# Nine warm-up products in place of eleven at the start of a mixer-and-MLP kernel

**The chip, the cores and the metric.** One core of one Trainium2 chip. The metric is device microseconds for one execution of the program. Engines: PE is TensorE's matmuls, PEld its weight loads, DVE VectorE, ACT ScalarE, POOL GpSimd, SP the engine that issues most DMAs. "Eleven" and "nine" stand for the kernel before and after.

## The reference, cut to what matters

```python
B, S, D, F = 1, 2048, 512, 1792                   # bf16
h  = gelu(layernorm(x) @ w1)                      # layer 1
hs = concat(four column groups of h, shifted by 1, -1, 2, -2 tokens) @ w2
x1 = x + hs
out = x1 + gelu(layernorm(x1) @ w3) @ w4          # layer 2
```

## The kernel before

Sixteen tiles of 128 tokens. A script fixes TensorE's order. The other engines' orders come from a list scheduler inside the kernel, with its own model of durations. The script begins:

```python
SCRIPT = """
warm:11 sa:0 sb:0 ty:1 ra:0 rb:0 ty:2 up1:1 th:0 up1:2 ty:3 mix:0-1 ty:5 ty:4 up1:3-4 ...
"""
LOADS = """
tp16 x1 x2 w1a w1b x3 x4-5 w2b w2a x8 x6 w3b w3a ... x0@act x12
"""
```

`warm:n` issues n products on a tile of zeros that nothing reads. `sa`, `sb` are the first and second pair of transposes of tile 0, each needing one normalised half of x. `ra`, `rb` are its four w1 products; the first two need the first half of w1 (`w1a`), the last two the second half (`w1b`). `ty:t` are transposes of tile t, `up1:g` the w1 product of a group, `th:0` the transposes back, `mix:t` the four w2 products of a tile.

```python
def warm_pe(n):
    b, v = next_bank()
    rows = zeros[:].unsqueeze(1).to_broadcast([P, 4, P])
    def f(e):
        for _ in range(n):
            ins = e.matmul(o_ps[:, b, :], zeros[:], rows, start=True, stop=True)
        return ins
    pg.add("pe", ..., f, reads=[(("zeros",), 0)], writes=[(("o", b), v)],
           dur=min(n, 7) * 427 + max(0, n - 7) * 216)          # the scheduler's model

# the four products of tile 0, in two halves (hh)
ins = e.matmul(y_ps[:, p, 0:D], xnT[:, dc, P*t : P*(t+1)], w1_sb[:, dc, :], start=(dc == 0), stop=(dc == DC-1))
# the mixing product of tile t
ins = e.matmul(dst, hT[:, j, c0 : c0+P], w2_sb[:, j, :], start=(j == 0), stop=(j == DC-1))
```

## Time and profile before

| | eleven |
|---|---|
| median of 3 runs | 135.48 us (135.25 to 135.73) |
| profiled execution | 135.97 us, span 134.6 us |
| TensorE busy | 132.4 us, 98% of the span |
| warm-up | eleven products, 0.44 to 5.1 us |
| full clock granted from | 6.44 us |
| layer 2's first product | 18.30 us |

The profiled execution is slower than the median: executions differ, and the first 10 us decide by how much. The last line is a good gauge, since from there TensorE runs nearly without a gap. Below, "start of layer 2" is that moment:

```profile
18.30 2.90 PE L641 MATMUL y_ps<-xnT,w_sb 128*128 128x128 bf16 x49
```

(From TensorE's timeline of eleven: start, length, what.) The lines that show the bound and the warm-up are in the prediction.

### The profile page before, as it was taken

What the parts mean: (1) busy time and instruction counts of PE and PEld (TensorE: products, weight loads), DVE (VectorE), ACT (ScalarE), POOL (GpSimd) and SP (SyncE); (2) the same over time, 40 slices, a digit from 0 to 9 for tenths busy, and PEclk for the clock granted to TensorE, in tenths of its full rate; (3) what the DMA queues carried; (4) which work ended last, traced back from release to release, by engine and by line L of the source; (5) the groups of instructions that cost most, each with busy time, mean ns of one, the idle gap of its engine ahead of it and who ended that gap; (6) DMA issues with size and microseconds to landing.
All of it is one profiled execution on the core that took longest, in us unless ns stands there. A gap on an engine that the chain in (4) does not pass through costs nothing.

```text
span 134.6 us, 2153 instructions
## 1 busy us (share of the span) xinstructions
PE 132.4 (98%) x847; PEld 73.1 (54%) x847; DVE 48.6 (36%) x147; ACT 62.1 (46%) x97; POOL 26.4 (20%) x61
## 2 busy tenths in 40 slices
PE   8999999999999999999999999999999999999994
PEld 3587779644656444444448844444444444444464
DVE  2689898863078810050007032232220000232222
ACT  6669829897544875557657542000006663000000
POOL 2444548963003650010003210000000000000000
PEclk9999999999999999999999999999999999999999
DMA  5999999955572135001000302111111000111112
GB/s 150 294 358 406 353 176 362 98 113 98 100 83 78 39 78 105 12 5 39 0 0 0 79 6 64 53 39 39 39 39 39 0 5 0 39 39 39 39 39 78
DMA packets 21369, 12.19 MB, mean 91 GB/s; under 512 B 13936, under 2 KB 20848, under 8 KB 21360
## 3 DMA queue, kind: packets, MB, share of 16 engines
q1 hardware_dynamic: 20784, 11.80, 35.0%
q10 hardware_dynamic: 576, 0.26, 0.7%
q8 instruction: 6, 0.10, 0.3%
q14 instruction: 3, 0.02, 0.1%
HBM read 6.82 MB, written 2.10 MB: 66 GB/s over the span
## 4 chain that ended last, share of the span: by engine, by line
PE 98%; DVE 0%; issue 0%; DVEq 0%
PE y_ps L641 46%; PE o_ps L710 36%; PE o_ps L681 10%; PE o_ps L735 4%; PE y_ps L505 2%; PE y_ps L543 1%; DVE o_sb L718 0%; PE o_ps L609 0%; DVE zeros L362 0%; DVEq L873 0%
## 5 line engine op out<-in xcount | busy, mean ns | idle before, releaser
L641 PE MATMUL y_ps<-xnT,w_sb 128*128 128x128 bf16 (+2 forms) x480 | 63.7, 292 | 0.0
L641 PEld LDWEIGHTS y_ps<-xnT,w_sb 128*128 128x128 bf16 x480 | 39.2, 98 | 24.2 <-DVE nmr L465 0.2
L710 PE MATMUL o_ps<-w_sb,h2T 128*128 128x512 bf16 (+3 forms) x252 | 48.9, 355 | 0.0
L656 ACT ACTIVATE h2T<-y_ps 128x1024 bf16<-128x1024 f32 (+2 forms) x29 | 28.7, 994 | 36.8 <-PE y_ps L641 36.8
L710 PEld LDWEIGHTS o_ps<-w_sb,h2T 128*128 128x128 bf16 x252 | 23.6, 98 | 25.2
L718 DVE TENSOR_TENSOR o_sb<-o_ps,x_sb 128x512 bf16<-128x512 f32 (+3 forms) x18 | 11.4, 631 | 43.3 <-PE o_ps L710 43.3
L681 PE MATMUL o_ps<-w_sb,hT 128*128 128x512 bf16 x64 | 15.4, 379 | 0.0
L438 POOL TENSOR_TENSOR rstd<-mv,neghalf 128x1 f32<-128x1 f32 x18 | 9.9, 554 | 26.8 <-DVE mv L433 25.0
L431 DVE BATCH_NORM_STATS2 st<-x_sb 128x6 f32<-128x512 bf16 x18 | 12.1, 675 | 2.7 <-DMA x_sb<-in_x_dram 2.7
L438 POOL TENSOR_TENSOR rstd<-vpe,neghalf 128x1 f32<-128x1 f32 x14 | 7.7, 557 | 26.2 <-DVE mv L420 14.1
L688 DVE SCALAR_TENSOR_TENSOR x_sb<-o_ps,x_sb 128x512 bf16<-128x512 f32 x10 | 6.9, 688 | 15.6 <-PE o_ps L681 15.6
L656 ACT ACTIVATE hT<-y_ps 128x512 bf16<-128x512 f32 (+1 forms) x10 | 8.1, 809 | 5.2 <-PE y_ps L641 5.2
L469 ACT ACTIVATE xn_buf<-x_sb,nmr,rstd 128x512 bf16<-128x512 bf16 x12 | 9.6, 806 | 1.9 <-POOL nmr L465 1.3
L415 ACT ACTIVATE junk<-x_sb 128x512 bf16<-128x512 bf16 x14 | 8.7, 623 | 3.7 <-DVE x_sb L688 3.4
L692 DVE TENSOR_TENSOR x_sb<-o_ps,x_sb 128x512 bf16<-128x512 f32 x6 | 4.1, 686 | 15.5 <-PE o_ps L681 15.4
L681 PEld LDWEIGHTS o_ps<-w_sb,hT 128*128 128x128 bf16 x64 | 6.1, 98 | 5.7 <-issue 0.2
L460 DVE TENSOR_SCALAR xn_buf<-x_sb,mv,rstd 128x512 bf16<-128x512 bf16 x12 | 5.3, 440 | 1.7 <-POOL rstd L438 1.3
L472 POOL TENSOR_SCALAR xn_buf<-x_sb,rstd,nmr 128x512 bf16<-128x512 bf16 x7 | 5.5, 784 | 0.6 <-DVE nmr L465 0.4
L735 PE MATMUL o_ps<-zeros 128*128 128x512 bf16 x11 | 4.9, 629 | 0.4 <-DVE zeros L362 0.4
L433 DVE BATCH_NORM_AGGREGATE mv<-st 128x2 f32<-128x9 f32 x18 | 3.2, 187 | 0.2
L505 PE MATMUL y_ps<-ident,xn_buf 128*128 128x128 bf16 x32 | 3.2, 242 | 0.0
L505 PEld LDWEIGHTS y_ps<-ident,xn_buf 128*128 128x128 bf16 x32 | 2.6, 110 | 1.1 <-issue 0.6
(34 smaller groups left out, 30.9 us busy)
## 6 DMA issues: line engine op xcount, KB each, us to landing
w_sb<-in_w_dram SPq DMA_DIRECT2D x4, 896.0 KB, 7.8
out_dram<-o_sb SPq DMA_DIRECT2D x15, 128.0 KB, 1.7
x_sb<-in_x_dram SPq DMA_DIRECT2D x9, 128.0 KB, 5.0
w_sb<-in_w_dram SPq DMA_DIRECT2D x4, 256.0 KB, 4.8
x_sb<-in_x_dram SPq DMA_DIRECT2D x3, 256.0 KB, 5.2
xnT<-xn_buf SPq DMA_TRANSPOSE x24, 2.5
x_sb<-in_x_dram ACTq DMA_DIRECT2D x1, 128.0 KB, 2.6
out_dram<-o_sb ACTq DMA_DIRECT2D x1, 64.0 KB, 1.6
```

Source lines behind the costliest of these rows:

```text
L415: (lambda d: (lambda e: e.activation(d, src, ACT_F.Square, accum_out=sums[:, q, 1:2])))(junk[:, b, :]),
L431: pg.add("dve", f"bnst{q}", lambda e: e.bn_stats(st9[:, q, 0:6], src), reads=rs, writes=[(("st", q), 0)], dur=605)
L438: lambda e: e.tensor_tensor(col(rstd), var, neghalf[:], ALU.pow),
L469: f = lambda e: e.activation(dst, src, ACT_F.Identity, bias=nmr[:, q : q + 1], scale=rstd[:, q : q + 1])
L505: ins = e.transpose(chunk(c), xn_buf[:, slot(q), P * c : P * (c + 1)], ident[:])
L641: ins = e.matmul(y_ps[:, p, W * i : W * (i + 1)], wsb[:, dc, P * fc : P * (fc + 1)], src[:, dc, P * t0 : P * t0 + W], start=(dc == 0), sto ...
L656: (lambda d, s: (lambda e: e.activation(d, s, ACT_F.Gelu_apprx_tanh)))(dst, ysrc),
L681: ins = e.matmul(dst, hT[:, j, c0 : c0 + P], w2_sb[:, j, :], start=(j == 0), stop=(j == DC - 1))
L688: f = lambda e: e.scalar_tensor_tensor(x1_sb[:, t, :], dst, 1.0, x_sb[:, t, :], ALU.mult, ALU.add, accum_out=sums[:, NT + t, 0:1])
L710: ins = e.matmul(dst, h2T[:, fc, P * t : P * (t + 1)], w4_sb[:, fc, cs], start=(fc == 0), stop=(fc == FC - 1))
L718: (lambda d, c: (lambda e: e.tensor_tensor(o_sb[:, oi, c], d, x1_sb[:, t, c], ALU.add)))(dst, cs),
L735: ins = e.matmul(o_ps[:, b, :], zeros[:], rows, start=True, stop=True)
```

## The change

Its intent: real work stands ready behind the last warm-up products, so let it in earlier.

```diff
-warm:11 sa:0 sb:0 ty:1 ra:0 rb:0 ty:2 up1:1 th:0 up1:2 ty:3 mix:0-1 ty:5 ty:4 up1:3-4 ty:6 mix:2 up1:5 ty:16
+warm:9 sa:0 sb:0 ty:1 ra:0 rb:0 ty:2 up1:1 th:0 up1:2 ty:3 mix:0-1 ty:5 ty:4 up1:3-4 ty:6 mix:2 up1:5 ty:16
```

## The prediction

> **What bounds the kernel now.** I read the page first (busy shares, then the chain that ended last), then the pieces of that chain in order of time, then the timeline of the first 10 us, because the change touches only the first instructions.
>
> The page's shares, its busy tenths for PE and its chain:
>
> ```profile
> PE 132.4 (98%) x847; PEld 73.1 (54%) x847; DVE 48.6 (36%) x147; ACT 62.1 (46%) x97; POOL 26.4 (20%) x61
> PE   8999999999999999999999999999999999999994
> PE 98%; DVE 0%; issue 0%; DVEq 0%
> ```
>
> TensorE is the bound from 0.44 us to the end: it alone is 98% of the chain, so a shift of its first real product moves the end by as much, unless a wait appears. The start of the chain, piece by piece (start, length, what):
>
> ```profile
> 0.44 4.87 PE o_ps L735 x11
> 5.31 0.85 PE y_ps L505 x8
> 6.17 1.06 PE y_ps L543 x4
> 7.23 0.22 PE y_ps L505 x4
> 7.45 0.89 PE y_ps L641 x16
> ```
>
> The first piece is the eleven warm-up products on zeros; nothing reads their result. Then come the transposes of tiles 0 and 1 (eight), four 512-column products for tile 0, the transposes of tile 2 (four) and the first w1 block. The weight loads give the issue spacing (start, length, what, idle before):
>
> ```profile
> 3.83 0.15 PEld L735 LDWEIGHTS o_ps<-zeros 128*128 128x128 bf16 x1 [0.28 <-issue]
> 4.26 0.15 PEld L735 LDWEIGHTS o_ps<-zeros 128*128 128x128 bf16 x1 [0.28 <-issue]
> 4.68 0.15 PEld L505 LDWEIGHTS y_ps<-ident,xn_buf 128*128 128x128 bf16 x1 [0.28 <-issue]
> 5.11 0.79 PEld L505 LDWEIGHTS y_ps<-ident,xn_buf 128*128 128x128 bf16 x7 [0.28 <-issue]
> ```
>
> They step by 0.427 us: all eleven products ran at the slow rate. The eleventh is issued at 4.68 and the first transpose product starts at 5.11. When were its operands there? The timeline again:
>
> ```profile
> 3.58 0.91 ACT L446 ACTIVATE xn_buf<-x_sb,mv 128x256 bf16<-128x256 bf16 x2
> 4.10 0.41 DVE L460 TENSOR_SCALAR xn_buf<-x_sb,mv,rstd 128x512 bf16<-128x512 bf16 x1
> 5.56 0.29 DVE L513 COPY xnT<-y_ps 128x256 bf16<-128x256 bf16 x1 [0.95 <-PE y_ps L505]
> 5.89 0.28 DVE L513 COPY xnT<-y_ps 128x256 bf16<-128x256 bf16 x1
> 6.16 0.41 DVE L460 TENSOR_SCALAR xn_buf<-x_sb,mv,rstd 128x512 bf16<-128x512 bf16 x1
> ```
>
> The two halves of tile 0 (ScalarE) ended at 4.08 and 4.49, tile 1 (VectorE) at 4.51. So the first transposes stood ready behind warm-up products for 0.6 to 1.0 us, and VectorE idled 0.95 us for them. That is what the change is after.
>
> **What the Trainium skill says.** "TensorE: Matmul & The Clock Gate", Part 1, says the array starts at half clock and is released after a busy window of about 3.4 us that runs freely, so the moment depends on where the first product falls in it; it gives 426.7 ns per 512-column product cold and 215.7 ns warm. The trace agrees: 427 ns for every warm-up product, 216 ns between the third and fourth tile-0 products. Its clock record starts full rate at 6.44 us, 6.0 us after the first product, and the spacing changes there. (The page's row of granted clock shows full speed throughout, having no earlier record.) The same page, Part 4, says transposes do not count as busy for this clock in the same way. Nothing here shows that: transposes fill 0.86 us of the 3.4 us before the release, and later ones run 56 ns apart, the full rate. I keep it as a risk.
>
> **The change part by part.** Two products go: 2 x 0.427 = 0.854 us of TensorE at the slow rate. The ninth then ends its issue at 0.441 + 9 x 0.427 = 4.28 instead of 5.11 to 5.14. That isn't the gain. The clock is released by time, not by count, so real work that moves forward moves into slow time. With the release at T and real work beginning at S before T, work worth (T-S)/2 of full-rate time is done at T, so the end goes as (T+S)/2: two products fewer are worth at most 0.854/2 = 0.43 us, whatever T is.
>
> Now with the waits of this trace, release kept at 6.44:
> 1. First two transposes of tile 0: ready 4.08, start 4.28, take 2 x 0.107, to 4.49.
> 2. Second two: the half ends at 4.48; with about 0.15 from an end to a TensorE start (the smallest slacks of this trace are 0.12 to 0.16) they start at 4.63. A new idle of 0.14. To 4.84.
> 3. Four of tile 1: ready, 4.84 to 5.27.
> 4. Tile-0 products 1 and 2 need the first copy (starts 4.73, ends 5.03) and half of w1, whose last piece landed at 5.08; TensorE itself is the latest, 5.27. At 0.427 each, to 6.12.
> 5. Products 3 and 4 need the other half of w1 (5.77) and the second copy (about 5.43): start 6.12. 0.32 us of the third is slow, its last quarter fast (0.05), then 0.216: to 6.71.
> 6. Tile 2's transposes start at 6.71 instead of 7.07; their operand (VectorE, behind both copies) ends near 5.83.
>
> Gain: 7.07 - 6.71 = **0.36 us**. Does it survive? I took the slack of each later TensorE block, its start less the end of its last operand. The tight ones are the transposes of the gelu of tile 0 (0.16), the w1 blocks of tile 2 (0.14) and tile 4 (0.12), and the first layer-2 transpose (0.13). All hang on ScalarE, VectorE and GpSimd work released by TensorE itself, which moves along. Fixed are the loads: tile 3 lands at 6.12 for statistics that began at 6.48 (room 0.36); the last of w2 at 8.96 for a product at 9.55, then 9.19 (0.23 left, about 0.1 after the hop); tile 6 at 9.61 for statistics at 10.05, then 9.69. From 18.3 us on slack is over 1 us at nearly every block (0.5 to 0.9 at three blocks from 36.7 to 40.1, fed by TensorE's own work; the tail pieces feed one another), so nothing later takes the gain back.
>
> In executions where the clock is released earlier, the gain is smaller. At T = 4.5 the eleven end at 4.83 and tile 2's transposes start near 6.44, held by copies and norms; with nine they start near 6.32, held by the second half of w1 (5.77 plus hop, then 2 x 0.216). That leaves 0.12, and w2 at 8.96 would take most of it. Between 0.1 and 0.36, I choose 0.25: 135.48 - 0.25 = 135.23, call it 135.25.
>
> **The rivals.**
> (a) *Loads take over and nothing is gained.* For: w1's second half and w2 are within 0.1 to 0.4 us of becoming the last operand. Against: in the profiled execution each still had room. Time 135.4 to 135.5.
> (b) *The clock is released a window later.* With nine products there is a hole of about 0.14 us near 4.5, and more of the deciding window is transposes. If that window no longer counts as busy, release slips about 3.4 us and the end by half, some 1.7 us less the 0.36: near 136.8. Against: the hole is 4% of the window. For: the first 2.6 us of products before 3.03, about three quarters of the window before the deciding one, did not release it, so some threshold above three quarters is possible. One in twelve.
> (c) *The list order of the other engines changes.* The kernel places instructions with its own model, in which the warm-up's length enters (products beyond seven at 216 ns: 0.43 us less). The order is tuned by a table of biases, so ScalarE, VectorE and GpSimd could be dealt differently. In that model, too, the second half of tile 0 holds TensorE, so later steps move little. For harm: slacks of 0.12 to 0.16 in the first 17 us. Against: over 1 us later. Plus or minus 0.3 us, rarely 1.
> (d) *The whole 0.85 us is gained*, if the release came earlier by as much. Against: nothing earlier is busy than before. 134.6.
>
> **Range and chances.** The three runs spread over 0.48 us, as a release at random times would make them (0.5 us per us of T); the median of a few moves by 0.2. Adding (a) to the upper side and (d) to the lower, and some of (b) and (c): 134.8 to 136.0. Two per cent is 2.7 us. A gain of that size exceeds all the products removed, and a loss needs (b) and a bad (c) together: faster 0.01, same 0.97, slower 0.02.
>
> **What would show each step right or wrong.** Nine weight loads of the warm-up 0.427 apart; the first transpose product near 4.28, a gap of 0.1 to 0.2 before the third, tile 2's transposes 0.1 to 0.4 us earlier at an equal release time; real products at 0.427 up to the release. The release should lie within 3.4 to 6.8 us of the first product; much later is (b). An idle stretch that a load ends, on TensorE near 5.8 or 9.0, is (a). A different sequence on VectorE or ScalarE is (c). I am wrong if equal release times give an equal or later end, or over 0.5 us gained.

## The result, and the profile after

Nine: 135.28 us median of 6 runs (135.20 to 135.41). Eleven beside it: 135.37 (135.01 to 137.26; the last is set aside as slow in the ratio, but counted in this median). The ratio is 0.9998, 95% interval 0.9978 to 1.0017: the same. A ratio here is the mean time of one kernel's runs over that of the other's of the same rounds, so it isn't quite the ratio of the medians quoted. Executions over 1.5% slower than the fastest of the same kernel are left out of the means.

Compared instruction by instruction, the orders of VectorE, ScalarE, GpSimd and SP are identical in both; on TensorE two products are missing. So rival (c), another order, is out.

The profiled execution of nine took 135.24 us, 0.73 less than that of eleven. That is *not* the effect of the change, as the weight loads show (start, length, what, idle before and what ended it):

```profile
3.41 0.15 PEld L735 LDWEIGHTS o_ps<-zeros 128*128 128x128 bf16 x1 [0.28 <-issue]
4.37 0.13 PEld L505 LDWEIGHTS y_ps<-ident,xn_buf 128*128 128x128 bf16 x2 [0.81 <-POOL rstd L438]
4.71 0.34 PEld L505 LDWEIGHTS y_ps<-ident,xn_buf 128*128 128x128 bf16 x6 [0.21 <-ACT xn_buf L446]
5.12 0.13 PEld L543 LDWEIGHTS y_ps<-w_sb,xnT 128*128 128x128 bf16 x2
5.68 0.11 PEld L543 LDWEIGHTS y_ps<-w_sb,xnT 128*128 128x128 bf16 x2 [0.43 <-DMA w_sb<-in_w_dram]
...
8.80 0.56 PEld L681 LDWEIGHTS o_ps<-w_sb,hT 128*128 128x128 bf16 x4 [0.20 <-issue]
```

Two things differ from eleven. First, the clock: in this execution it was released between 3.84 (the ninth warm-up product) and 4.41 us, since the first transposes already run 0.055 us apart; in the execution of eleven it was released at 6.44. Second, waits that eleven did not have. The weights of the third tile-0 product wait for w1 (last piece landed at 5.63). At 8.80 the first mixing product comes late too: TensorE's sequencer stands in a wait from 8.27 to 8.77 that ends with the last of w2 (landed at 8.74); the view says only "issue". So a gain was there and loads stepped into it.

A trap in reading: the page's chain of nine, and its first long pieces, name something else.

```profile
PE 91%; DMA 3%; DVE 2%; issue 1%
```

```profile
2.08 3.92 DMA x_sb<-in_x_dram
...
8.43 0.61 DVE st L431
9.04 1.67 PE o_ps L681 x7
```

(The first fence is the chain by engine, the second the chain in order of time.) It blames tile 3's load and the statistics of tile 4. But the line says x7 where two tiles of four products make eight: the record of the first mixing product is missing. Its weights were loaded at 8.80, so it started near 8.83, and the chain, starting from the second product at 9.04, took a VectorE instruction that had ended at 9.03 for its releaser. The mixing products read nothing from it.

Layer 2 began at 17.57:

```profile
17.57 3.62 PE L641 MATMUL y_ps<-xnT,w_sb 128*128 128x128 bf16 x62
```

From there to the end both executions are equal: 135.97 - 18.30 = 117.67 and 135.24 - 17.57 = 117.67. Whatever the change does, it does before 18 us.

### The profile page after: what moved, and what is told of

Read it like the earlier page. It is cut to its first block, busy times and chain, and to the rows that moved or that the text cites. A ratio compares the mean times of both kernels' runs of the same rounds, so it can differ in the third digit from the quotient of the medians.

```text
span 133.9 us, 2137 instructions
## 1 busy us (share of the span) xinstructions
PE 130.8 (98%) x833; PEld 72.3 (54%) x845; DVE 48.8 (36%) x147; ACT 62.3 (47%) x97; POOL 26.4 (20%) x61
## 2 busy tenths in 40 slices
DMA packets 21369, 12.19 MB, mean 91 GB/s; under 512 B 13936, under 2 KB 20848, under 8 KB 21360
## 4 chain that ended last, share of the span: by engine, by line
PE 91%; DMA 3%; DVE 2%; issue 1%
PE y_ps L641 45%; PE o_ps L710 36%; PE o_ps L681 10%; DMA x_sb<-in_x_dram 3%; DVE st L431 1%; PE y_ps L505 1%; DVE hT L619 0%; DVE mv L433 0%; DVE xn_buf L460 0%; DVE o_sb L718 0%; DVE xnT L513 0%
## 5 line engine op out<-in xcount | busy, mean ns | idle before, releaser
L681 PE MATMUL o_ps<-w_sb,hT 128*128 128x512 bf16 x58 | 14.3, 379 | 0.5 <-DVE st L431 0.3
L735 PE MATMUL o_ps<-zeros 128*128 128x512 bf16 x9 | 4.0, 631 | 0.4 <-DVE zeros L362 0.4
L427 DVE SCALAR_TENSOR_TENSOR vpe<-sums,mv 128x1 f32<-128x1 f32 x14 | 2.2, 158 | 2.7 <-ACT junk L415 2.4
L423 DVE TENSOR_SCALAR mv<-mv 128x1 f32<-128x1 f32 x14 | 2.9, 210 | 0.3
```

The source lines that it names most:

```text
L681: ins = e.matmul(dst, hT[:, j, c0 : c0 + P], w2_sb[:, j, :], start=(j == 0), stop=(j == DC - 1))
```

## The experiments

**Theory (loads).** Where the clock is released early, nine is held by w1's second half and w2, and the gain goes into that wait; where it is released late, nine is some 0.4 us ahead. **Rivals.** (norms) The two halves of tile 0's normalisation hold TensorE, no load does. (nothing) The products weren't on the path at all. (full) Each product costs its whole 0.427 us.

Twelve runs in three groups of four, each group on one chip (the first and the third on the same); eleven ran beside each group. In kernels with moved loads or foreign weights the compute engines' orders were kept as they were, and compared. The table has the profiled executions, in us. "Release" is where the spacing of products turns from 0.427 to 0.216 (or of transposes from 0.107 to 0.056), or the clock record where there is one; "w1" the landing of the last piece of its second half; "third" the start of the third tile-0 product.

| run | release | w1 | third | start of layer 2 | that less w1 | time |
|---|---|---|---|---|---|---|
| eleven (before) | 6.44 | 5.77 | 6.64 | 18.30 | 12.52 | 135.97 |
| nine (after) | 3.84-4.41 | 5.63 | 5.68 | 17.57 | 11.94 | 135.24 |
| nine_again | 3.51 | 6.28 | 6.33 | 18.00 | **11.72** | 135.77 |
| nine_third | 6.29 | 5.61 | 6.00 | 17.80 | 12.19 | 135.50 |
| nine_fourth | 6.30 | 5.61 | 5.95 | 17.78 | 12.18 | 135.44 |
| nine_free | 4.79 | 5.70 | 5.58 | 17.37 | 11.67 | 135.04 |
| eleven_free | 5.56 | 5.20 | 6.44 | 18.10 | 12.91 | 135.78 |
| thirteen | 3.89 | 6.14 | 6.19 | 17.86 | **11.72** | 135.67 |
| none | 7.03 | 5.13 | 5.69 | 17.98 | 12.84 | 135.67 |
| nine_x2act | 4.34 | 6.01 | 6.06 | 17.73 | **11.72** | 135.49 |
| eleven_x2act | 5.50 | 5.41 | 6.43 | 18.09 | 12.68 | 135.76 |
| nine_w1act | 3.64 | 4.25 | 6.54 | 18.20 | 13.95 | 135.87 |
| nine_latew1 | 5.76 | 6.79 | 6.83 | 18.50 | **11.72** | 136.17 |
| eleven_latew1 | 5.02 | 6.77 | 6.81 | 18.48 | **11.72** | 136.16 |

In bold: the third product waited for w1's second half, and no later load held.

The time less the start of layer 2 is 117.66 to 117.81 in all fourteen; the span (first to last instruction) less it is 116.34 to 116.35. So the start of layer 2 settles the span almost exactly, and the rest of the time lies outside the span.

Release and landing may not be independent. In the nine traces with w1's second half at its usual place, the two earliest releases known to 0.1 us (3.51 and 3.89) go with the two latest landings (6.28 and 6.14), and releases from 4.79 on with 5.13 to 5.77. That is too little to show a link, and no run sets the one without the other.

### First group: the change again, loads taken off the path, two products more

**nine_again** (no edit; the changed kernel).

> The changed kernel once more, beside eleven on the same chip. Loads theory (the gain is lost because the second half of w1, then the last of w2, become the last operand when the clock is released early): over 5 rounds 0.0 to 0.2 us under eleven, scatter smaller than that of eleven; TensorE waits for the w1 load before the third tile-0 product and for the w2 load before the first mixing product, unless the release is late (after 5.5 us), when it is 0.36 us ahead of eleven at equal release. Rival (nothing was ever on the path: the tile-0 norm halves alone hold TensorE): no wait on a load.

Measured: 135.44 median (135.01 to 135.77), eleven beside it 135.64; ratio 0.9983 (0.9951 to 1.0014).

```profile
5.66 0.11 PEld L543 LDWEIGHTS y_ps<-w_sb,xnT 128*128 128x128 bf16 x2 [0.72 <-DMA w_sb<-in_w_dram]
6.32 0.11 PEld L543 LDWEIGHTS y_ps<-w_sb,xnT 128*128 128x128 bf16 x2 [0.55 <-DMA w_sb<-in_w_dram]
```

(Weight loads of nine_again.) With a release at 3.51 both halves of w1 hold TensorE. The second landed at 6.28, against 5.77 in the trace that I predicted from, though it was issued at the same time. The first mixing product waited for no load this time (w2 at 8.83, product at 9.25). The runs spread over half of eleven's range (0.76 against 1.57 us), but eleven's highest, 136.64, has an ordinary span of 134.1: by spans it is 0.6 against 0.8. In nine_third, below, it is 1.5 against 0.8, the other way round, so the smaller scatter that I expected isn't established. The earliest release of all didn't give the best time. The rival "norms" falls: it allows no wait on a load.

**nine_free** (other weights for tile 0, so wrong there): the third and fourth tile-0 products take the first half of w1 again, the first mixing product takes w1 for w2.

```diff
-warm:11 sa:0 ...
+warm:9 sa:0 ...
-w1_sb[:, dc, :]                 # tile 0's products
+w1_sb[:, dc % 2, :]
-w2_sb[:, j, :]                  # mixing
+(w1_sb if t == 0 else w2_sb)[:, j, :]
     pg.order()
+    for op in pg.ops:            # the waits follow what is really read
+        if op.name == "mix0":    op.reads = [w1's chunks in place of w2's, the rest as it was]
+        if op.name == "rows0_1": op.reads = [w1's first two chunks in place of the last two, the rest as it was]
```

> Nine, but the third and fourth tile-0 products and the first mixing product take weights that landed earlier (a wrong result for tile 0, on purpose; orders of all engines unchanged). Loads theory: the waits at 5.63 and 8.74 go, and it ends 0.2 to 0.4 us before nine_again (ratio 0.997 to 0.9985) when the release is early. Rival (norms and copies hold TensorE): within 0.1 us of nine_again.

Measured: 135.15 median (134.83 to 135.34); ratio to eleven 0.9963 (0.9933 to 0.9993), the only one of nine's family whose interval is clear of 1. Against nine_again of the same rounds: 0.9963 / 0.9983 = 0.998, or 0.27 us, as expected in size, but at the edge of the noise (six runs each; an interval of about 0.3 us either way). The trace shows the wait gone:

```profile
5.12 0.56 PEld L543 LDWEIGHTS y_ps<-w_sb,xnT 128*128 128x128 bf16 x4 [0.17 <-DMA w_sb<-in_w_dram]
```

All four weight loads run in one row; the third product started at 5.58, ahead of the landing at 5.70. Layer 2 began at 17.37, the earliest of all.

**eleven_free**: the same edit on eleven.

> Eleven, with the same two loads taken off the path. Loads theory: eleven hardly waits for them, so 0 to 0.1 us under eleven, and 0.25 to 0.4 us over nine_free. If instead the loads hold eleven as much as nine, it falls by as much as nine_free does.

Measured: 135.77 median (135.11 to 136.05); ratio 0.9999 (0.9961 to 1.0037). Taking the loads away gives eleven nothing measurable and nine 0.27 us: its means are 0.5 us apart from nine_free's (135.64 and 135.12; by spans 0.47), a little over the 0.25 to 0.4 expected. That difference is clear of noise (0.52 us, give or take about 0.4). So with these loads off the path the two products are worth about half a microsecond. That the loads take this back in the unedited kernels is what the waits in the traces say; the timed difference of 0.27 us alone would not prove it.

**thirteen** (the scheduler's model of the warm-up kept at eleven, so that orders stay).

```diff
-warm:11 sa:0 ...
+warm:13 sa:0 ...
-           dur=min(n, 7) * 427 + max(0, n - 7) * 216)
+           dur=7 * 427 + 4 * 216)
```

> Thirteen warm-up products with the order of all engines as with eleven. By the rule of (T+S)/2 each product beyond those hidden costs 0.216 us at the end whatever the release: 0.43 us over eleven (ratio 1.003), less if a load still held eleven. Rival (products cost 0.427 each): 0.85 us over. Rival (warm-up is hidden by loads altogether): nothing.

Measured: 135.82 median (135.13 to 136.31); ratio 1.0014 (0.9979 to 1.005). Between nothing and the 0.43 us expected; not told apart. Its profiled execution says why the cost is blurred:

```profile
3.81 0.78 PEld L735 LDWEIGHTS o_ps<-zeros 128*128 128x128 bf16 x4 [0.28 <-issue]
...
6.18 0.11 PEld L543 LDWEIGHTS y_ps<-w_sb,xnT 128*128 128x128 bf16 x2 [0.40 <-DMA w_sb<-in_w_dram]
```

The release came at 3.89, the last four warm-up products ran at full rate, and w1 (6.14) held TensorE all the same. Thirteen and nine_again, both released early, differ at the start of layer 2 by 18.00 - 17.86 = 0.14, exactly the difference of their w1 landings (6.28 - 6.14), *with four more warm-up products in the earlier one*. The rival "full" (0.85 us) isn't seen.

### Second group: loads moved, and no warm-up

**nine_third** (no edit).

> Nine once more, as the partner of the other three on this chip, and for another release and another arrival of w1. Loads theory: 0 to 0.3 us under eleven; in the profile the third tile-0 product or the first mixing product starts within 0.1 us of a landing, if the release was before 5.5 us.

Measured: 135.33 median (135.09 to 136.51); ratio 0.9990 (0.9938 to 1.0043). This execution has a late release, 6.29, close to the 6.44 of eleven's trace:

```profile
4.19 0.89 PEld L505 LDWEIGHTS y_ps<-ident,xn_buf 128*128 128x128 bf16 x8 [0.63 <-POOL rstd L438]
...
5.65 0.10 PEld L543 LDWEIGHTS y_ps<-w_sb,xnT 128*128 128x128 bf16 x1 [0.35 <-DMA w_sb<-in_w_dram]
6.00 0.15 PEld L543 LDWEIGHTS y_ps<-w_sb,xnT 128*128 128x128 bf16 x1 [0.24 <-issue]
6.35 0.43 PEld L505 LDWEIGHTS y_ps<-ident,xn_buf 128*128 128x128 bf16 x4 [0.20 <-issue]
```

The third product started 0.39 after w1's landing, with no wait for it: its weight load (5.65) did wait, but TensorE was still at the second product. Layer 2 began at 17.80, 0.50 before eleven's:

```profile
17.80 3.40 PE L641 MATMUL y_ps<-xnT,w_sb 128*128 128x128 bf16 x58
```

Half of the release's 0.15 us explains 0.08; 0.42 is the change. nine_fourth, below, repeats it: release 6.30, 17.78, so 0.52 - 0.07 = 0.45. So the rival "nothing" falls at a late release. Both are set against the one trace of eleven, though.

Two of nine_third's timed runs, 136.51 and 136.25, have spans of 135.2 and 134.9, longer than all 33 of eleven's in these groups (133.7 to 134.7). They have no trace. As an estimate, a release near 8 us (by (T+S)/2) or w1 landing near 7 us (by the 11.72) would each explain them; which it was stays open.

**nine_x2act**: tile 2 of x is issued from ScalarE's queue, to let w1 and all later loads go out earlier. The result is correct.

```diff
-tp16 x1 x2 w1a w1b x3 ...  x0@act x12
+tp16 x1 w1a w1b x3 ...  x0@act x2@act x12
```

> Nine, with tile 2 of x issued from the ScalarE queue, so that both halves of w1 and all later loads are issued some 0.45 us earlier (correct result; compute orders unchanged). Loads theory: w1 lands 0.3 to 0.45 us earlier, the waits on loads shrink or go, and it ends 0.15 to 0.35 us before nine_third (as nine_free did: 0.27 us in the mean). Rival (the 0.27 us was scatter): within 0.1 us of nine_third.

Measured: 135.43 median (134.98 to 136.00); ratio 0.9978 (0.9938 to 1.0017), not to be told from nine_third. The move didn't do what it was made for: the first half of w1 landed at 3.60, but the second at 6.01, and held TensorE again.

```profile
6.05 0.11 PEld L543 LDWEIGHTS y_ps<-w_sb,xnT 128*128 128x128 bf16 x2 [0.72 <-DMA w_sb<-in_w_dram]
```

So the run does not speak against the loads theory, but it shows no remedy either.

**eleven_x2act**: the same edit on eleven.

> Eleven with the same move. Loads theory: 0 to 0.15 us under eleven, and 0.25 to 0.4 us over nine_x2act, since now the two products show. If loads hold eleven as they hold nine: as much faster as nine_x2act is over nine.

Measured: 135.90 median (135.33 to 136.86); ratio 1.0015 (0.9971 to 1.0059). Nothing gained for eleven, and 0.5 us over nine_x2act in the mean (135.96 and 135.45). But the 136.86 has 2.4 us outside its span, against 1.3 to 1.4 in the others; by spans it is 0.35, within the 0.25 to 0.4 expected, and not clear of noise.

**none**: no warm-up at all.

```diff
-warm:11 sa:0 ...
+sa:0 ...
```

> No warm-up product at all. If the release needs about 3 to 6 us of products before it, as in the six traces so far (3.43 to 6.44 us from the span's start, first product at 0.44), it comes at 7.3 to 10.3, and the end is 1.2 to 2.2 us later (ratio 1.009 to 1.016), real products at 0.427 us and transposes at 0.107 until then. Rival (the warm-up does not matter to the release): as nine, within 0.2 us.

(The 3.43 is a slip: the earliest release of those six is 3.51.) Measured: 136.31 median (135.67 to 137.13); ratio 1.0046 (0.9999 to 1.0092). The direction was right; the size, 0.62 us (0.85 by spans), was about half of the least that I had expected. TensorE's timeline:

```profile
3.91 1.13 PE L505 MATMUL y_ps<-ident,xn_buf 128*128 128x128 bf16 x8 [3.91 <-ACT xn_buf L446]
4.84 1.91 PE L543 MATMUL y_ps<-w_sb,xnT 128*128 128x512 bf16 x4
6.54 0.62 PE L505 MATMUL y_ps<-ident,xn_buf 128*128 128x128 bf16 x4
6.97 0.53 PE L641 MATMUL y_ps<-xnT,w_sb 128*128 128x128 bf16 x6
```

All work to 6.97 ran slow, and the release came at 7.03, 3.1 us after the first product. This profiled execution is the fastest of none's six; a release as late after the first product as in eleven's trace (6.0 us) would be at 9.9, and half the 2.9 us more would make 137.1. The six runs fill just that range. My 1.2 to 2.2 us had probably left out that a kernel with warm-up is itself held by loads when it is released early; no run tests that.

### Third group: one load earlier, one load later

**nine_fourth** (no edit).

> Nine once more, partner of the other three. In the three traces of nine whose third tile-0 product waited for w1, layer 2 began 11.72 us after the second half of w1 had landed (6.28 to 18.00, with six parts of x2act 6.01 to 17.73), or 0.2 later when w2 also held it; the time of the profiled execution is that start plus 117.7. Expected: 135.0 to 135.7, and the start of layer 2 at the larger of w1's landing plus 11.72 and a clock path of 17.4 to 17.8.

(The text has a slip: the three traces meant are nine_again, nine_x2act and thirteen, as in the table.)

Measured: 135.53 median (134.94 to 135.75); ratio 0.9977 (0.9940 to 1.0014). The start of layer 2, 17.78, is on the clock path, w1 plus 11.72 being only 17.33.

**nine_w1act**: the second half of w1 is issued from ScalarE's queue right after tile 0. The result is correct.

```diff
     pg.order()
+    moved = next(op for op in pg.seq if op.name == "dma_w1b")
+    pg.seq.remove(moved)
+    ahead = next(op for op in pg.seq if op.name == "dma_x0")
+    pg.seq.insert(pg.seq.index(ahead) + 1, moved)
+    moved.eng, moved.start = ahead.eng, ahead.start
```

> Nine, with the second half of w1 issued from the ScalarE queue right after tile 0, about 0.85 us earlier, and all later loads 0.45 us earlier (correct result, compute orders unchanged). Loads theory: that half no longer holds TensorE; 0.15 to 0.35 us before nine, 0.2 to 0.5 us before eleven. If it only pushes the first half of w1 or tile 0 back by as much (shared transfer rate): within 0.1 us of nine or slower.

Measured: 135.34 median (134.92 to 135.87); ratio 0.9969 (0.9930 to 1.0009), not told from nine_fourth. In the profiled execution the second half landed at 4.25 and the *first* at 6.05, so the wait only changed its half. Layer 2 began at 18.20, which is that landing plus 11.72 plus the 0.43 of the two further products that now come after it (2 x 0.216):

```profile
6.09 0.55 PEld L543 LDWEIGHTS y_ps<-w_sb,xnT 128*128 128x128 bf16 x4 [1.34 <-DMA w_sb<-in_w_dram]
```

**nine_latew1**: the second half of w1 is issued two loads later (the same five lines, behind the load of tile 4).

> Nine, with the second half of w1 issued two loads later, about 1 us (correct, compute orders unchanged). Loads theory: TensorE waits for it in every execution, layer 2 begins 11.7 us after its landing, about 18.4 to 18.7, and it ends near 136.2 (135.9 to 136.7).

**eleven_latew1**: the same edit on eleven.

> Eleven with the same delay. Loads theory: the two products are hidden wholly behind the load: within 0.15 us of nine_latew1. Rival (products are on the path whatever the loads do): 0.3 to 0.45 us slower than nine_latew1.

Measured: nine_latew1 136.16 median (135.78 to 136.45), as expected, ratio 1.0025 (0.9989 to 1.0061); eleven_latew1 136.38 (136.16 to 137.07), ratio 1.0053 (1.0011 to 1.0095). Their profiled executions, nine_latew1 first:

```profile
6.83 0.11 PEld L543 LDWEIGHTS y_ps<-w_sb,xnT 128*128 128x128 bf16 x2 [1.45 <-DMA w_sb<-in_w_dram]
...
18.50 2.68 PE L641 MATMUL y_ps<-xnT,w_sb 128*128 128x128 bf16 x45
```

```profile
6.81 0.11 PEld L543 LDWEIGHTS y_ps<-w_sb,xnT 128*128 128x128 bf16 x2 [0.89 <-DMA w_sb<-in_w_dram]
...
18.48 2.73 PE L641 MATMUL y_ps<-xnT,w_sb 128*128 128x128 bf16 x46
```

With the load late, nine waits 1.45 us and eleven 0.89, and both begin layer 2 at the same time, 11.72 after the landing: the two products are hidden wholly. That held for the profiled pair. The timed means differ by 0.33 us (136.12 and 136.45; 0.20 without eleven's 137.07), more than the 0.15 that I had allowed, and in the range that I had given the rival (0.3 to 0.45); by spans it is 0.30. Six runs each can't tell 0.33 from 0.15 or from none (about 0.37 either way). A late release together with an early landing would leave part of the gain; the timed runs have no traces, so this stays open.

### The four comparisons of nine and eleven together

The ratios are 0.9998, 0.9983, 0.9990 and 0.9977. Each interval contains 1; all four lie below, with a mean of 0.9987, or 0.18 us. That is no proof of a gain, and it bounds it: a few tenths of a microsecond at most.

Even this mean flatters nine. The record gives the span of 111 of the timed runs. Time less span is 1.27 to 1.47 us in 104 of them; the seven others (1.62 to 2.75) are all runs with eleven warm-up products, four of them among the 33 plain ones at 2.5 or more. Why is not known, but the extra time lies outside the program's instructions. By spans, nine is 0.12 us below eleven in nine_again, 0.05 above in nine_third and 0.16 below in nine_fourth: 0.08 us in the mean, give or take 0.2.

## Why the prediction was right, point by point

- **Same, near 135.25.** Right: 135.28, within the range. That it came so close is partly luck: in the repeats nine's median was 135.33 to 135.53, and the 135.25 lay between a late and an early release whose shares nobody knew. The forecast gain of 0.25 us is compatible with the four ratios (0.18 us in the mean) and the spans (0.08), but so is no gain at all.
- **Two cold products are worth 0.43 us, not 0.85, as the end goes with (T+S)/2.** Right where no operand waits. With S the first real product: eleven at (6.44 + 5.11)/2 = 5.78; nine_third at (6.29 + 4.26)/2 = 5.28, nine_fourth at (6.30 + 4.24)/2 = 5.27; none at (7.03 + 3.91)/2 = 5.47. The differences to eleven are 0.50, 0.51 and 0.31; the starts of layer 2 differ by 0.50, 0.52 and 0.32. In eleven_free (5.34) it is off: 0.44 expected, 0.20 measured, because transposes at the full rate end before their copies and TensorE then waits for these, 0.23 us before the first tile-0 product. I had used the rule "whatever T is"; it holds for late releases.
- **0.36 us at an equal release.** Slightly low: 0.42 and 0.45. The mis-sized term is the 0.15 us from an operand's end to TensorE's start: it measured 0.05 (the norm half ended at 4.47 and the transpose began at 4.53 in nine_third; 4.66 and 4.71 in nine). The idle of 0.14 us before the second pair of transposes was 0.05 in nine_third and absent in nine_fourth, where the norm half ended at 4.40 and not at 4.48.
- **At an early release w1 and then w2 take the gain** (0.12 us or less left). Right in kind, seen at 5.68 and 8.80 in the profile after. The 0.12 itself was not measured: no trace shows the unedited eleven with an early release. The weak step was "Fixed are the loads", taken from one trace: among the nine traces of kernels that issue w1's second half at its usual place, ahead of tile 3 and behind tile 2 and the first half, it landed anywhere from 5.13 to 6.28 us. In nine_again it landed 0.65 us later than in the trace after; there w2 held 0.22 us on top, so layer 2 began 0.43 us later, with the earlier release of the two. Rival (a) is therefore not a rival, but what happens in executions with an early release or a late landing.
- **The release within 3.4 to 6.8 us of the first product** (an estimate: one to two of the 3.4 us windows that the prediction cites). The lower edge was off: 3.1 in nine_again; the latest was 6.0 (eleven).
- **Rival (b), a release pushed out by a window.** Not seen in a trace: nine's five with usual loads released between 3.51 and 6.30, eleven's two at 5.56 and 6.44. For the two long runs of nine_third it isn't excluded. **(c)** Not seen: equal orders. **(d)** Not seen: the profiled 0.73 us less was an earlier release.

What is shown: the wait on w1 and its price (11.72 us from its landing to layer 2 in five traces, with nine, eleven and thirteen products), the gain of 0.42 to 0.45 us at a late release (two traces of nine against one of eleven), and that with both loads off the path nine is faster than eleven (0.52 us in time, 0.47 by spans). What is only argued: that the loads take back just what nine gains in the timed runs, how often each case occurs there, since only profiled executions show it, and whether an early release and a late landing belong together.

## What to carry to other kernels

Here a warm-up product that ran at half clock cost at most about half its length (0.42 to 0.45 us for two of 0.427), since what took its place ran at half clock too. Before counting on an earlier start, look for the next operand to arrive, and take its arrival from several traces: here the release of the clock and the landing of a load each wander by more than the whole gain. Two single profiles of such kernels (0.73 us apart here) say nothing about the change until both have been set to the same release.

## What the Trainium skill lacked or had wrong

- "TensorE: Matmul & The Clock Gate", Part 1, gives the transition as around 4 us of sustained activity, give or take 0.5. Here it came 3.1 us (nine_again, none) to 6.0 us (eleven) after the first product. The free-running window that the same part describes, and its note that the count of cold products varies from run to run, fit such a spread better than its ±500 ns. As 3.1 us is less than the 3.4 us of one window, a window busy for nine tenths must have been enough, if the window is as the page says.
- The same page, Part 4, says full clock does not engage for transposes and that they don't count as busy in the same way. Here transposes ran 0.056 us apart after the release and 0.107 before it, and in none, where eight transposes fill most of the first 0.93 us and four more follow, the release came 3.1 us after the first of them; the four real products between them fill only 1.7 us of that. The kernel calls `e.transpose`; the trace names these MATMUL and does not show whether the transpose mode of that page was on.
- No page that I used states how much one load's landing wanders from one execution to the next: 5.13 to 6.28 us for the second half of w1, issued at 1.46 to 1.47 in the traces with the usual load order.
